# The first expert's first two row tiles, read two batches early and multiplied between the last batch's tasks

## The chip, the cores and the metric

The kernel runs on one core of one Trainium2 chip. The metric is the time of one execution on the device, in microseconds (us). The kernel before takes 782.67 us, the median of 3 runs that lie between 782.0 and 784.62 us. The profile used here is of one execution whose first and last instruction are 782.3 us apart.

Five engines work side by side: TensorE (PE; its weight loads are listed apart as PEld), VectorE (DVE), ScalarE (ACT), GpSimd (POOL) and SyncE (SP, which here only starts transfers). Each works through its own instructions in order and waits on semaphores for the others. 16 DMA engines move the data.

## What is computed

Attention with a sliding window and a linear distance bias, followed by a mixture of experts in which every row goes to one expert.

```python
# attention: q, k, v of (8 batches, 8 heads, 576 positions, 64)
scores = q @ k.T / sqrt(64); bias = -slope[h] * abs(rel)
mask = (rel >= 0) & (rel < 128)
attn = softmax(where(mask, scores + bias, -1e9)); attn_out = attn @ v
# bridge: x of (4608 rows, 512)
logits = x @ w_gate                       # (4608, 8)
expert_idx = argmax(logits, axis=1); gate_w = softmax(logits)[expert_idx]
for e in range(8):                        # w1[e]: (512, 1024), w2[e]: (1024, 512)
    rows = expert_idx == e
    y[rows] = maximum(x[rows] @ w1[e], 0) @ w2[e]
out = gate_w[:, None] * y
```

With the inputs used, the eight experts get 547, 614, 590, 502, 618, 462, 608 and 667 rows. The first expert already has 425 rows after the 27 tiles of 128 rows that the first six batches fill; its 256th row lies in the 16th tile.

## The kernel before

All arithmetic is in float32. The first stage works through 32 units (8 batches x 4 pairs of heads). What turns a finished batch into rows for the experts is a list of tasks (gate logits, transposes, choice of the expert, place of each row, scaling of the row, sending it off); a few tasks are put between the parts of each later unit. Each finished row is written by an indirect DMA into `x_rows`, a table in memory with a stretch for each expert; a row has 512 values, its own number and its gate weight.

```python
def row(ts, i):                      # one tile of 128 rows
    ...
    for hp in range(HP):
        nc.tensor.transpose(m[...], xT[pair][:, hp, c : c + P], ident[:])
    nc.vector.tensor_tensor(xs[:, i % RG, :Dm]..., m[:], rs_all[:, t, :]..., op=ALU.mult)
def send(ts, i):
    scatter(ts[i], xs_of.pop(ts[i])[:, i % RG, :])          # indirect DMA into x_rows
...
for u in range(NU + 1):                                     # NU = 32 units
    ...
    do(0 if slow else 1)
    ...
    do(len(tasks) if u == NU else 0 if slow else 2 if len(tasks) < 14 else 3)
```

The second stage handles 15 groups in turn: for each expert its first 512 rows (4 tiles), and between two experts one tile of 128 rows that some expert has over. A group of 4 tiles is multiplied with Strassen's seven products (`seven1` for the first layer, in two halves, `seven2` for the second); a group of one tile is done plainly (`layer1`, `layer2`).

```python
for i, g in enumerate(groups):
    after = groups[i + 1 : i + 3] + [None, None]
    if after[0] is not None:
        gather(after[0])                              # xg, two buffers: x_rows -> SBUF
        after[0]["w2"] = load_w2(after[0]["src"][1])
    if g["n"] == NJ:
        if i == 0:
            turn(g, [0, 1]); ...                      # the first group's products
            ...                                       # in an order of their own
        seven1(g, 0, ...); seven1(g, 1, ...)
        if i == 0: check_range(first)
    else:
        layer1(g)
    tokens(g)                                         # row numbers, masked -> si
    if after[1] is not None: get_w1(after[1])
    if after[0] is not None:
        turn(after[0], range(after[0]["n"]))          # transposes of the next group's xg
        ...
    if g["n"] == NJ: seven2(g, ...)                   # send_out of its 4 tiles inside
    else: layer2(g)
def send_out(g, j, row):
    ins = nc.gpsimd.indirect_dma_start(
        out=out[:, :], out_offset=bass.IndirectOffsetOnAxis(ap=g["si"][:, j : j + 1], axis=0),
        in_=row, in_offset=None, bounds_check=N - 1, oob_is_err=False)
def tokens(g):                                        # si = (row number & mask0) | mask1
    g["si"] = pools["u"].tile([P, NJ], I32, name="si")
    ...
def gather(g):
    xg = g["xg"] = pools["x"].tile([P, NJ, RW], F32, name="xg")   # bufs=2
    for j0, j1 in ((0, 2), (2, n)) if n > 2 else ((0, n),):
        nc.sync.dma_start(xg[:, j0:j1, :], src[:, j0:j1, :])
```

Of the kernel before, what the change touches and what calls it, by code (L numbers as in the profile page):

```python
# [21 lines left out]
def kernel(  # L22
# [49 lines left out]
    nc.gpsimd.memset(ones_sq[:], 1.0)  # L72
    zero_e = consts.tile([P, E], F32, name="zero_e")
# [51 lines left out]

    def start_routing():
        for sel in sels:
            nc.vector.memset(sel[:], 0.0)
        nc.vector.tensor_copy(sels[n_routed[0] % 2][0:1, :, 0], region[0:1, :])
# [21 lines left out]
    def place(tiles, tmp_pool, ps, name):  # L151
# [17 lines left out]
        if tiles[-1] == NT - 1:  # L169
            nc.vector.tensor_sub(cnt[:], rk[:, :, GT], region[:])  # L170

# [24 lines left out]

    expert_w = {}
# [137 lines left out]

    order_all = ExitStack()
# [12 lines left out]
    k_lo = [P * j for j in range(KT)] + [S - P]  # L349
    with tc.tile_pool(name="tab", bufs=1) as tab, \  # L350
         tc.tile_pool(name="ld", bufs=2) as ld, \
# [8 lines left out]
        rel_i = tab.tile([P, 2 * P], I32, name="rel_i")  # L360
        nc.gpsimd.iota(rel_i[:], pattern=[[1, 2 * P]], base=0, channel_multiplier=-1)
        rel = tab.tile([P, 2 * P], F32, name="rel")
        nc.gpsimd.tensor_copy(rel[:], rel_i[:])
# [3 lines left out]
        for h in range(H):  # L367
            nc.vector.tensor_scalar_mul(fac[:, h, :], rel[:], 2.0 ** (-8.0 * (h + 1) / H))
# [25 lines left out]
        q_sb, k_sb, v_sb, xT, lT, sT = {}, {}, {}, {}, {}, {}  # L394
        probs, exps, mgs, sums = {}, {}, {}, {}

        def load(b):
            q_sb[b] = ld.tile([P, HP, S], F32, name="q_sb")
            k_sb[b] = ld.tile([P, HP, S], F32, name="k_sb")
            v_sb[b] = ld.tile([P, KT + 1, Dm], F32, name="v_sb")  # L400
            cols = slice(b * S, (b + 1) * S)
            step = 1 if b == 0 else HP
            for c in range(0, HP, step):
                nc.sync.dma_start(q_sb[b][:, c : c + step, :], qT3[:, c : c + step, cols])
                nc.sync.dma_start(k_sb[b][:, c : c + step, :], kT3[:, c : c + step, cols])
                if c == 0:
                    nc.sync.dma_start(
                        v_sb[b][:, :KT, :], v[b * S : b * S + KT * P, :].rearrange("(t p) d -> p t d", p=P)
                    )
                    nc.sync.dma_start(v_sb[b][:, KT, :], v[(b + 1) * S - P : (b + 1) * S, :])  # L410

        def scores(u):
# [3 lines left out]
            for j, c, q0, n in BLK:  # L416
                s, c = divmod(c, W // 2)
                for par in range(2):
                    half = slice(par * HALF, (par + 1) * HALF)
                    nc.tensor.matmul(  # L420
                        sps[s][par][:, c : c + n], lhsT=k_sb[b][half, hp, k_lo[j] : k_lo[j] + P],
                        rhs=q_sb[b][half, hp, q0 : q0 + n], start=True, stop=True,
                    )
# [150 lines left out]
        def tasks_of(b):  # L574
# [7 lines left out]
            return ts + [lambda: [send(tiles, i) for i in (len(tiles) - 2, len(tiles) - 1)]]  # L582

        load(0)
        load(1)
# [8 lines left out]
        for u in range(NU + 1):  # L594
# [3 lines left out]
            if u < NU:  # L598
                if hp == 1 and 1 < b + 1 < NB:
                    load(b + 1)  # L600
                if 0 < u <= E:
                    clear_rows(u - 1)
                if u == NU // 2:
                    expert_w[0] = load_w1(moe_w1[0]), load_w2(moe_w2[0])
                scores(u)
                factors(u, 0)
            do(0 if slow else 1)
# [3 lines left out]
            if u > 0:  # L611
# [3 lines left out]
                if hp == 0:  # L615
                    tasks += tasks_of(b - 1)
            do(len(tasks) if u == NU else 0 if slow else 2 if len(tasks) < 14 else 3)

    xe = rte.tile([1, NX], I32, name="xe")
    n_more = rte.tile([1, 3], F32, name="n_more")
    n_more_i = rte.tile([1, 3], I32, name="n_more_i")
    xr = rte.tile([1, NX], I32, name="xr")
    masks = rte.tile([P, 2, E, NJ], I32, name="masks")
    xmasks = rte.tile([P, 2, NX], I32, name="xmasks")

    def extras():
        with tc.tile_pool(name="route", bufs=1) as sm:

            def to_masks(out, has):
                nc.vector.tensor_scalar_mul(out[:, 0], has, -1.0)
                nc.vector.tensor_scalar(
                    out[:, 1], has, scalar1=-float(2 * N), scalar2=float(2 * N), op0=ALU.mult, op1=ALU.add,
                )

            has = sm.tile([P, E, NJ], F32, name="has")
            nc.vector.tensor_tensor(
                has[:], cnt[:].unsqueeze(2).to_broadcast([P, E, NJ]), tail[:, None, :].to_broadcast([P, E, NJ]),
                op=ALU.is_gt,  # L640
            )
            to_masks(masks, has[:])
            og = sm.tile([P, E, NX], F32, name="og")
            nc.vector.tensor_tensor(
                og[:], cnt[:].unsqueeze(2).to_broadcast([P, E, NX]), thr[:, None, :].to_broadcast([P, E, NX]),
                op=ALU.is_gt,
            )
            ovt = sm.tile([P, E], F32, name="ovt")
            nc.vector.reduce_sum(ovt[:], og[:], axis=AX)
            ove = sm.tile([P, E], F32, name="ove")  # L650
            nc.vector.tensor_tensor_scan(ove[:], ovt[:], zero_e[:], 0.0, op0=ALU.add, op1=ALU.add)

            done = sm.tile([P, NX, E], F32, name="done")
            mine = sm.tile([P, NX, E], F32, name="mine")
            k3 = kx[:].unsqueeze(2).to_broadcast([P, NX, E])
            nc.vector.tensor_tensor(done[:], ove[:, None, :].to_broadcast([P, NX, E]), k3, op=ALU.is_le)
            nc.vector.tensor_sub(ovt[:], ove[:], ovt[:])
            nc.vector.tensor_tensor(mine[:], ovt[:, None, :].to_broadcast([P, NX, E]), k3, op=ALU.is_le)
            nc.vector.tensor_sub(mine[:], mine[:], done[:])
            xe_f = sm.tile([1, NX], F32, name="xe_f")  # L660
            nc.vector.reduce_sum(xe_f[:], done[0:1], axis=AX)
            nc.vector.tensor_scalar_min(xe_f[:], xe_f[:], float(E - 1))

            off = sm.tile([P, NX, E], F32, name="off")
            at = sm.tile([P, NX], F32, name="at")
            nc.vector.tensor_sub(off[:], k3, ovt[:, None, :].to_broadcast([P, NX, E]))
            nc.vector.tensor_scalar(off[:], off[:], scalar1=float(NJ), scalar2=float(P), op0=ALU.add, op1=ALU.mult)
            nc.vector.tensor_mul(off[:], off[:], mine[:])
            nc.vector.reduce_sum(at[:], off[:], axis=AX)

            num = sm.tile([P, NX], F32, name="num")
            nc.vector.tensor_mul(mine[:], mine[:], cnt[:, None, :].to_broadcast([P, NX, E]))
            nc.vector.reduce_sum(num[:], mine[:], axis=AX)
            base = sm.tile([P, NX], F32, name="base")
            nc.vector.scalar_tensor_tensor(base[:], in0=num[:], scalar=-float(P), in1=at[:], op0=ALU.add, op1=ALU.min)
            nc.vector.tensor_scalar_max(base[:], base[:], 0.0)
            xr_f = sm.tile([1, NX], F32, name="xr_f")
            nc.vector.scalar_tensor_tensor(
                xr_f[:], in0=xe_f[:], scalar=float(N), in1=base[0:1, :], op0=ALU.mult, op1=ALU.add,
            )  # L680
            nc.vector.tensor_scalar_min(xr_f[:], xr_f[:], float(E * N - P))
            nc.vector.tensor_copy(xr[:], xr_f[:])
            nc.vector.tensor_scalar(base[:], base[:], scalar1=tail[:, 0:1], scalar2=None, op0=ALU.add)
            nc.vector.tensor_tensor(at[:], base[:], at[:], op=ALU.is_ge)
            nc.vector.tensor_tensor(num[:], num[:], base[:], op=ALU.is_gt)
            nc.vector.tensor_mul(num[:], num[:], at[:])
            to_masks(xmasks, num[:])
            nc.vector.tensor_copy(xe[:], xe_f[:])
            nc.vector.tensor_scalar_min(n_more[:, 0:1], ove[0:1, E - 1 :], float(NX))

    def check_range(first):
        with tc.tile_pool(name="range", bufs=1) as sm:
            if first:
                inr = sm.tile([P, NT * H], F32, name="inr")
                n_in = sm.tile([P, 1], F32, name="n_in")
                sums = rs_all.rearrange("p t h -> p (t h)")
# [383 lines left out]
```

## Time and profile before

| what | value |
| --- | --- |
| time, median of 3 | 782.67 us |
| PE busy | 711.7 us (91% of the span) |
| PEld, DVE, ACT, POOL busy | 587.7, 405.3, 220.7, 175.8 us |
| 60 to 195 us (units and tasks) | PE busy 127.06 of 135.00 us |
| 226.5 to 308.4 us (seam, first expert) | PE busy 57.03 of 81.90 us, granted clock 0.83 |
| 439.3 to 504.6 us (one tile over, one expert) | PE busy 64.60 of 65.30 us, granted clock 1.00 |
| moved by DMA | 130.74 MB, mean 167 GB/s |

The page cuts the span into 40 slices of 19.6 us and gives the busy share of each engine in tenths; the row PEclk gives the clock that TensorE was granted, in tenths of full speed. Lines of a timeline give start, duration, engine, source line, operation, tiles and, in brackets, how long the engine had been idle before and what ended that. Lines of a table of waits give the total, the number and the longest of the waits of one kind. A float32 matmul shows as two entries.

### The profile page before, as it was taken

To read this page: it belongs to the slowest core of one execution; us is meant where nothing else is said; L and a number is where in the kernel's file an instruction comes from. 1 tells how busy PE (TensorE), PEld (TensorE's weight loads), DVE (VectorE), ACT (ScalarE), POOL (GpSimd) and SP (SyncE) were. 2 spreads that over 40 slices of the span, in tenths; PEclk is the share of its full clock that TensorE was granted. 3 is DMA by queue.
4 is the path that set the end of the run, shared out by engine and by line. 5 is a ranking of instruction groups with operands and counts; after the bars stand their busy time and mean duration, and the time that the engine had idled before them with its cause. 6 is when DMAs were issued, how large, how long until landed. Compare 5 with 4: busy or idle time off the path is not lost.

```text
span 782.3 us, 11598 instructions
## 1 busy us (share of the span) xinstructions
PE 711.7 (91%) x4678; PEld 587.7 (75%) x4678; DVE 405.3 (52%) x696; ACT 220.7 (28%) x506; POOL 175.8 (22%) x186
## 2 busy tenths in 40 slices
PE   5899899999944879999999999999999999998992
PEld 4677667777634769788788878978878887896881
DVE  4457787777756734463363454436346345443620
ACT  4455555546411112121211212112122121211210
POOL 4446665776630002000200200100020020010001
PEclk9999999999965999999999999999999999999996
DMA  9995895571126021912842482192275348205001
GB/s 332 364 354 195 275 345 168 182 242 56 42 97 245 35 108 41 366 60 89 296 159 108 150 302 108 32 350 76 103 280 175 107 146 308 108 30 189 1 1 58
DMA packets 53615, 130.74 MB, mean 167 GB/s; under 512 B 3503, under 2 KB 3503, under 8 KB 53552
## 3 DMA queue, kind: packets, MB, share of 16 engines
q1 hardware_dynamic: 47024, 110.97, 41.2%
q0 software_dynamic: 6000, 18.92, 6.4%
q8 instruction: 39, 0.64, 0.3%
q14 instruction: 24, 0.20, 0.1%
q10 hardware_dynamic: 528, 0.02, 0.0%
HBM read 102.55 MB, written 28.12 MB: 167 GB/s over the span
## 4 chain that ended last, share of the span: by engine, by line
PE 50%; issue 9%; DMA 5%; DVE 4%; POOL 1%; ACT 1%; SPq 0%; POOLq 0%; DVEq 0%
PE b L783 18%; PE a L783 13%; PE c L783 12%; PE c L941 5%; DMA xg<-x_rows 5%; ACT zo L853 1%; PE tp L909 1%; DVE zo L872 1%; POOL out_dram L880 1%; PE a L909 0%; DMA x_rows<-xs,slots 0%; PE b L909 0%; DVE hs L745 0%; DVE w1s L745 0%; DVE w1s L746 0%
## 5 line engine op out<-in xcount | busy, mean ns | idle before, releaser
L880 POOL DMA_INDIRECT out_dram<-zo,si x32 | 33.8, 1055 | 403.2 <-ACT zo L853 398.3
L420 PE MATMUL sp<-q_sb,k_sb 64*128 64x256 f32 (+2 forms) x640 | 73.0, 373 | 8.9 <-DMA k_sb<-in_kT_dram 5.0
L420 PEld LDWEIGHTS sp<-q_sb,k_sb 64*128 64x128 f32 x640 | 64.0, 202 | 20.5 <-issue 5.6
L427 ACT ACTIVATE e<-sp 128x512 f32<-128x512 f32 x128 | 66.2, 600 | 44.5 <-PE sp L420 44.4
L446 POOL TENSOR_TENSOR mg<-probs 128x768 f32<-128x768 f32 x31 | 57.7, 1860 | 73.2 <-DVE probs L439 37.9
L434 DVE TENSOR_TENSOR probs<-e,fac 128x1024 f32<-128x1024 f32 x32 | 47.0, 1468 | 44.1 <-ACT e L427 29.3
L783 PE MATMUL a<-xgT,w 128*128 128x256 f32 x256 | 62.6, 390 | 7.5 <-DVE xgT L911 7.5
L783 PEld LDWEIGHTS a<-xgT,w 128*128 128x128 f32 x256 | 50.2, 197 | 18.1 <-issue 11.2
L465 PE MATMUL m<-probs,v_sb 128*64 128x256 f32 (+3 forms) x768 | 63.2, 313 | 0.3 <-DVE xs L566 0.2
L783 PE MATMUL b<-xTs,w1s 128*128 128x256 f32 x256 | 60.6, 379 | 0.5 <-DVE u L813 0.5
L853 ACT ACTIVATE zo<-zo,xg 128x256 f32<-128x256 f32 x48 | 21.8, 501 | 136.5 <-DVE zo L864 89.4
L465 PEld LDWEIGHTS m<-probs,v_sb 128*64 128x64 f32 x768 | 47.9, 137 | 16.3 <-issue 2.3
L783 PE MATMUL a<-w,h_sb 128*128 128x256 f32 x256 | 59.3, 386 | 0.0
L783 PE MATMUL b<-w2s,hs 128*128 128x256 f32 x256 | 57.9, 379 | 0.0
L783 PEld LDWEIGHTS a<-w,h_sb 128*128 128x128 f32 x256 | 49.2, 195 | 6.6
L783 PEld LDWEIGHTS b<-xTs,w1s 128*128 128x128 f32 x256 | 48.6, 190 | 7.4 <-DVE u L813 0.9
L783 PEld LDWEIGHTS b<-w2s,hs 128*128 128x128 f32 x256 | 48.6, 190 | 6.6
L941 PE MATMUL c<-w,h_sb 128*128 128x512 f32 x112 | 49.2, 592 | 0.0
L173 POOL DMA_INDIRECT x_rows<-xs,slots x36 | 43.4, 1205 | 19.6 <-DVE cnt L170 8.2
L439 DVE TENSOR_TENSOR probs<-e,fac 128x1024 f32<-128x1024 f32 x32 | 42.3, 1321 | 0.4 <-ACT e L427 0.4
L813 DVE TENSOR_TENSOR u<-b,p 128x512 f32<-128x512 f32 x16 | 11.1, 691 | 52.7 <-PE b L783 52.7
L941 PEld LDWEIGHTS c<-w,h_sb 128*128 128x128 f32 x112 | 20.7, 190 | 23.4 <-issue 23.4
(198 smaller groups left out, 1137.7 us busy)
## 6 DMA issues: line engine op xcount, KB each, us to landing
w<-in_moe_w_dram SPq DMA_DIRECT2D x30, 2048.0 KB, 11.6
x_rows<-zero_row SPq DMA_DIRECT2D x8, 1028.0 KB, 15.0
xg<-x_rows SPq DMA_DIRECT2D x16, 514.0 KB, 4.6
v_sb<-in_v_dram SPq DMA_DIRECT2D x8, 1024.0 KB, 7.9
q_sb<-in_qT_dram SPq DMA_DIRECT2D x7, 1152.0 KB, 7.2
k_sb<-in_kT_dram SPq DMA_DIRECT2D x7, 1152.0 KB, 10.2
v_sb<-in_v_dram SPq DMA_DIRECT2D x8, 256.0 KB, 8.3
xg<-x_rows SPq DMA_DIRECT2D x7, 257.0 KB, 3.8
```

Of the source, the lines that this page charges most:

```text
L173: ins = nc.gpsimd.indirect_dma_start(out=x_d[:, :], out_offset=bass.IndirectOffsetOnAxis(ap=slots[:, t : t + 1], axis=0), in_=row, in_offs ...
L420: nc.tensor.matmul(sps[s][par][:, c : c + n], lhsT=k_sb[b][half, hp, k_lo[j] : k_lo[j] + P], rhs=q_sb[b][half, hp, q0 : q0 + n], start=Tru ...
L427: nc.scalar.activation(exps[u][s][:, par, :], sps[s][par][:], AF.Exp, scale=D ** -0.5)
L434: nc.vector.tensor_tensor(to.rearrange("p a (j c) -> p a j c", c=2 * P), e.rearrange("p a (j c) -> p a j c", c=2 * P), fac[:, heads, None, ...
L439: nc.vector.tensor_tensor(to, e[:], fac2[:, heads, :], op=ALU.mult)
L446: eng.tensor_add(mg[:, :, : 3 * P].rearrange("p a (t c) -> p a t c", c=P), two[:, :, :, 0, :], two[:, :, :, 1, :],)
L465: nc.tensor.matmul(xp[par * HALF : (par + 1) * HALF, lo - q0 : hi - q0], lhsT=v_sb[b][:, j, h * D : (h + 1) * D], rhs=probs[u][:, par, c + ...
L783: nc.tensor.matmul(out_of[:, i, :], lhsT=lhs(i, k), rhs=rhs(k), start=(first and i == 0 and k == 0), stop=(k == nk - 1), skip_group_check= ...
L813: nc.vector.tensor_add(u2[:], bb, p1[:])
L853: nc.scalar.activation(o[:, th, dh, i, :], src[:, i, :], AF.Copy, scale=g["xg"][:, j, Dm + 1 :])
L880: ins = nc.gpsimd.indirect_dma_start(out=out[:, :], out_offset=bass.IndirectOffsetOnAxis(ap=g["si"][:, j : j + 1], axis=0), in_=row, in_of ...
L941: nc.tensor.matmul(zf, lhsT=g["h"][:, fb, :P], rhs=g["w2"][:, fb, :], start=(fb == 0), stop=(fb == FB - 1))
```

## The change

The first expert's group is split. Its first two tiles (256 rows) are read from `x_rows` as soon as the first six batches are in it, two batches before the end, and are multiplied plainly, not with Strassen's products: their first layer between the tasks of the last batch, where TensorE waits, and their second layer after the last task, while the last rows travel to memory and back. The group's other two tiles follow as a plain group of two. If the first expert should have fewer than 256 rows by then, the two tiles are done again at the end.

To make room in SBUF for the new tiles, q and k are loaded for each unit (five buffers) instead of each batch (two buffers). The row numbers for the output are taken straight from the gathered rows (`ids_of_rows`), for all groups but those of one tile; the masks for full groups are gone, because unused rows of the table already hold a number out of range. The single-tile groups get their own transposed tile and hidden layer (`xT2`, `h2`), ACT does all their ReLUs, and the routing sums (`extras`) move ahead of the second stage.

```diff
+    def ids_of_rows(g, j):
+        return g["xg"].bitcast(I32)[:, j, Dm : Dm + 1]
+    def ids_masked(g, j):
+        return g["si"][:, j : j + 1]
     def send_out(g, j, row):
-            out=out[:, :], out_offset=bass.IndirectOffsetOnAxis(ap=g["si"][:, j : j + 1], axis=0),
+            out=out[:, :], out_offset=bass.IndirectOffsetOnAxis(ap=g["ids"](g, j), axis=0),
 ...
+            if tiles[-1] + 1 == early_end:
+                ts.append(lambda: early.update(early_group()))
+        def early_group():
+            g = dict(n=EJ, apart=True, ids=ids_of_rows, xg=plain.tile([P, EJ, RW], F32, name="xg2"))
+            nc.sync.dma_start(g["xg"][:], x_d[: EJ * P, :].rearrange("(j p) r -> p j r", p=P))
+            g["w1"], g["w2"] = expert_w[0]
+            return g
+        def last_tasks():
+            g = early
+            full = lambda: ps_s.tile([P, W // 2], F32, name="sp")
+            turns = [lambda j=j: turn(g, [j], full()) for j in range(EJ)]
+            hid = [lambda fb=fb: layer1(g, fb, ps_m.tile([P, S - 2 * P], F32, name="m")) for fb in range(FB)]
+            ts = tasks_of(NB - 1)
+            more = {2: turns, 6: hid[:3], 8: hid[3:4], 9: hid[4:5], 10: hid[5:6], 11: hid[6:]}
+            for i, task in enumerate(ts):
+                task()
+                for step in more.get(i + 1, ()):
+                    step()
+            extras(tab.tile([P, H, W // 2], F32, name="fac2").rearrange("p h c -> p (h c)"))
+            for j in range(EJ):
+                layer2(g, j, full(), ex.tile([P, 2, W // 2], F32, name="e").rearrange("p a c -> p (a c)")[:, :Dm])
 ...
-            do(0 if slow else 1)
+            do(0 if slow else 1 if b < NB - 1 else 2)
 ...
-            do(len(tasks) if u == NU else 0 if slow else 2 if len(tasks) < 14 else 3)
+            do(0 if slow else 2 if len(tasks) < 14 and b < NB - 1 else 3)
+        do(len(tasks))
+        last_tasks()
 ...
     def experts(first):
+            j0 = EJ if first and e == 0 else 0
             groups.append(dict(
-                n=NJ, e=e, rows=lambda e=e: x_d[e * N : e * N + CAP, :], mask=masks[:, :, e, :], apart=True,
+                n=NJ - j0, e=e, rows=lambda r=e * N + j0 * P, n=NJ - j0: x_d[r : r + n * P, :], ids=ids_of_rows,
+                apart=True,
             ))
 ...
-            tokens(g)
+            if "mask" in g:
+                tokens(g)
```

## The prediction

> **What bounds the kernel now.** I read the page's slices first:
>
> ```profile
> PE   5899899999944879999999999999999999998992
> PEclk9999999999965999999999999999999999999996
> ```
>
> TensorE is full from 40 us on, but for one hole in slices 12 to 14: the seam between attention and experts, where its clock drops too. The busy times by stretch size the hole and show that what follows is dense (columns after the length: PE, PEld, DVE, ACT, POOL, then clock, DMA share, GB/s):
>
> ```profile
> 226.50:308.40 81.90, 57.03 (x247) 48.31 (x247) 41.18 (x82) 11.04 (x20) 4.77 (x7) 0.83 0.29 107
> 373.60:439.30 65.70, 64.72 (x325) 54.86 (x324) 30.02 (x45) 13.51 (x27) 5.22 (x6) 1.00 0.48 167
> ```
>
> PE's waits in the seam:
>
> ```profile
> PE tp L909 <- DMA xg<-x_rows: 10.7, 1, 10.7
> PE a L783 <- DVE xgT L911: 7.5, 1, 7.5
> PE tp L703 <- DVE n_in L701: 4.6, 1, 4.6
> ```
>
> First PE waits for the last rows to reach memory and come back, then for the routing sums on DVE, then for the range check. From 308.4 us on a period (one tile over, then one expert) takes 65.2 to 65.7 us with under 1 us idle. There one more thing must be read: how close the next gather comes to being late. From PE's waits after 310 us and the timeline around 375 us:
>
> ```profile
> PE a L909 <- DMA xg<-x_rows: 3.6, 6, 1.0
> ...
> 374.55 0.91 ACT L853 ACTIVATE zo<-zo,xg 128x256 f32<-128x256 f32 x2 [2.55 <-DVE zo L872]
> 375.48 0.89 SPq L895 DMA_DIRECT2D xg<-x_rows  x2
> 376.80 0.97 POOL L880 DMA_INDIRECT out_dram<-zo,si  x1 [0.30 <-DVE h_sb L933]
> 380.76 1.04 PE L909 MATMUL tp<-ident,xg 128*128 128x128 f32 x8
> 382.78 0.63 PE L909 MATMUL a<-ident,xg 128*128 128x128 f32 x4 [0.98 <-DMA xg<-x_rows]
> 383.68 7.03 PE L941 MATMUL c<-w,h_sb 128*128 128x512 f32 x16
> ```
>
> The gather for the next expert goes out at 375.48, as soon as ACT has used the gate weights in the buffer's old rows. Its first half is just in time for the transposes at 380.76, its second half late by up to 1 us, six times. **The gather has no slack at all.** The fourth send of the old expert starts after it, at 376.80.
>
> **What the Trainium skill says.** "TensorE: Matmul & The Clock Gate", in its part 1 on the HAM clock gate, has PE at half clock after an idle window of about 3.4 us and full again after about as long busy. The trace agrees, and is harsher: after the 2.4 us idle before 222.07 us, 16 transposes at 222.91 took 3.65 us, while 8 take 1.04 at full clock; after 4.6 us idle, 16 matmuls at 282.80 took 5.04 us instead of 3.62. "DMA: Bandwidth & Descriptors", in the anatomy of one DMA on the gpsimd path, puts most of the fixed 2 us into the receipt from memory, without which the semaphore doesn't fire. Agreed: the last scatter starts at 229.63, its data have moved by about 231.9, and it lands at 232.94. "Perfetto Trace Analysis", on the most-contended engine, reads the same bubble repeated for a stretch as a shortage of buffers; that is my worry here.
>
> **The change, part by part.** Prices at full clock, from the timeline: a plain first-layer block of 256 rows is 8 entries of 128x256, as one product (1.73 us); 8 blocks are 13.8 us. The second layer of one tile is 16 entries of 128x512: 6.87 us; of two, 13.7. Transposing two tiles: 1.04.
>
> *Arithmetic.* Strassen for four tiles is 14 x 1.73 + 7 x 3.45 = 48.4 us; plain, twice 27.5 = 55.1. So PE gets 6.7 us more work.
>
> *The tail of attention.* The last unit's matmuls end at about 215.9 us. In the built order follow two logits (1.4), 8 early transposes (1.0), the gate's transposes (1.6), a row (0.45), three first-layer blocks (5.2), then the placing of rows, where PE waited 2.4 us before and now doesn't: about 225.7. Placing (0.7), four rows (0.45 each), three blocks between them and two after: 225.7 + 0.7 + 1.8 + 5 x 1.73 = 236.9, against 226.6 before. The second layer then runs to L = 250.6.
>
> *The wait for the rows.* It should lie behind that second layer, but doesn't. In the built program the gather of tiles 2 and 3 waits for the two early sends of outputs to land (its buffer lies where their tiles lay). So after L: ACT's weighing 0.15 + 0.69, POOL 0.15 later, landing 3.4 (the scatter at 229.63 took 3.31, the one at 225.72 3.5), SP's start 0.43 (232.94 to 233.37), gather 3.85 (233.37 to 237.22): PE starts at 259.3, at half clock.
>
> *Tiles 2 and 3.* Transposes 1.9 (as at 237.22), last copy 0.9, first layer 13.8 + 0.7 for the slow clock, one tile's transposes 0.5, second layer 13.7: the first tile over starts at 259.3 + 31.5 = 290.8. Before: 308.4. **Saved: 17.6 us.** The waits for DVE's sums are gone, because plain products need none; the sums for expert two run behind a single tile's work, and its w1 has been asked for 14 us earlier.
>
> *What it adds everywhere.* `ids_of_rows` makes each send read its row numbers from `xg` itself. A buffer that a transfer reads can't be overwritten until the transfer has landed, and in the built program the gather of each next expert now waits for all four sends of the last one, where before it waited for ACT and for `si`. So in each period the gather goes out not at 375.48 but at 376.80 + 3.4 + 0.43 = 380.6: 5.1 us later, on a transfer without slack. First half at 380.6 + 3.9 = 384.5 instead of 380.76: PE idles 3.7 us, enough to lose its clock. Four tiles' transposes at half clock take 3.8, so the single tile's second layer starts at 388.4 to 388.7 instead of 383.68: **4.9 us for each of six experts, 29.4 us.** For the second expert only one send comes after the last matmul: gather out at T + 1.0 + 3.4 + 0.43, first half at T + 8.7, where PE is ready at T + 7.15; with the half clock, 2.3 us.
>
> *No time:* masks removed, ReLUs moved, own tiles for single-tile groups (nothing in PE's waits names them), loads by unit (four units ahead, 18 us in the fast first units, against 7 to 10 us from issue to landing; after the first matmul PE never waits for q or k). The redo at the end doesn't run: 425 rows are there, 256 needed.
>
> Sum: 782.7 - 17.6 + 2.3 + 29.4 = 796.8.
>
> **Rivals.**
> 1. *The seam is all that counts* (the sends land in time, or one slow gather is absorbed): 782.7 - 17.6 = 765; if moreover the wait for rows did hide behind the second layer, 757. For it: the seam is the only hole in the page. Against it: the wait is in the built order, and six late second halves show that nothing is left to absorb.
> 2. *The send lands later than I think.* The median of all sends is 6.7 us to landing, the worst 8.5. Those ran beside weight loads; in the new order gather and weights wait behind the sends, so 3.4 to 4.2 (an early send of the last expert took 4.2) is what I choose. At 4.2, 0.8 more in seven places, 802; at 6.7, about 820.
> 3. *The tail doesn't fill.* DVE or POOL bounds the last two units, with five tasks a unit (PE waited 8.1 us in all for POOL's `mg`), or early loads collide with the clearing of `x_rows`: a few us more, 800 to 803.
>
> **Range and chances.** The per-period price dominates: 3.5 to 6.5 us gives 788 to 806. The seam's saving I trust to 4 us. Taken together I predict 797, 787 to 807. The line of 2% slower lies at 798.3, 1.5 us above my sum, so same and slower are nearly even; the errors that I can name lean upward, but the sum lies below. Faster by 2% needs rival 1.
>
> **What would show it.** Right: PE's waits hold about six of 3.5 to 5 us on the gather and a clock below 1.0 after each; SP waits for landed sends, not for ACT; periods of about 70 us instead of 65.3; the first single tile near 291 us, after 8 to 9 us idle between early second layer and the transposes of tiles 2 and 3. Wrong: periods still at 65, which would mean that the wait ends earlier than the landing; or a hole before 237 us, which would mean that the tail isn't filled.

## The result and the profile after

The changed kernel takes 787.53 us, the median of 4 runs (786.75 to 788.78), against 782.46 us for the kernel before on the same chip. The ratio is 1.0061, with a 95% interval of 1.0038 to 1.0084. The change costs about 5 us, a third of the 14.3 us that were predicted; the time lies at the lower edge of the predicted range (787 to 807 us). In the two profiled executions the spans differ by 3.2 us (785.5 against 782.3), and the sums below refer to these.

Most of the hole in the seam is closed, and small holes have opened behind it. The slices of the page:

```profile
PE   5899999999798799998999899899989989998992
PEclk8999899999999699999999999999999999999996
```

The two slices with a 4 have gone. From slice 19 on, every few slices an 8 stands among the 9s, where before there was none until the fourth slice from the end. The busy times by stretch of the changed kernel (the columns as in the prediction's table) give both sizes:

```profile
226.50:293.00 66.50, 57.63 (x204) 37.99 (x202) 17.36 (x50) 8.59 (x19) 9.03 (x10) 0.90 0.38 139
359.10:428.40 69.30, 66.42 (x325) 56.02 (x324) 28.70 (x39) 14.49 (x31) 5.28 (x6) 0.98 0.45 159
428.40:497.30 68.90, 66.35 (x325) 56.52 (x324) 28.69 (x39) 14.49 (x31) 5.25 (x6) 0.98 0.45 159
```

The seam up to the first single tile (a tile over from some expert) ends at 293.0 us instead of 308.4. The two periods shown, each from one single tile to the next, take 69.3 and 68.9 us where the same two took 65.7 and 65.4 before, with 2.9 and 2.6 us without a matmul and a clock of 0.98. PE's waits from 226 to 790 us:

```profile
PE tp L441 <- DMA xg<-x_rows: 23.6, 8, 7.9
PE a L450 <- DVE xT L443: 0.9, 1, 0.9
PE a L441 <- DMA xg<-x_rows: 0.7, 2, 0.4
```

The waits for the last rows, for DVE's sums and for the range check (10.7, 7.5 and 4.6 us before) have become one of 7.9 us in the seam, and the other seven of the first line are new: 0.7 us for the second expert and 2.3 to 2.6 us for each of six later ones. What SP's gathers (`xg`) wait for, from 300 us on, names the cause:

```profile
SPq L981 <- DMA out_dram<-zo,xg: 153.0, 7, 30.0
...
SPq L981 <- ACT zx L462: 64.8, 6, 11.6
```

In the kernel before, the first of these lines was

```profile
SPq L895 <- ACT zo L853: 164.3, 7, 26.7
```

that is, the weighing of the rows with the gate on ACT. Now it is the landing of a send, a transfer to the output. The total means nothing, because SP has little else to do; what counts is the releaser. The timeline of one period of the changed kernel shows the order:

```profile
360.05 0.91 ACT L950 ACTIVATE zo<-zo,xg 128x256 f32<-128x256 f32 x2 [2.55 <-DVE zo L969]
...
362.30 0.98 POOL L416 DMA_INDIRECT out_dram<-zo,xg  x1 [0.30 <-ACT h L454]
...
365.24 0.89 SPq L981 DMA_DIRECT2D xg<-x_rows  x2
...
368.99 1.11 PE L441 MATMUL tp<-ident,xg 128*128 128x128 f32 x8 [2.56 <-DMA xg<-x_rows]
```

ACT has used the gate weights at 360.96, as in the kernel before; yet the gather leaves at 365.24, after the fourth send (362.30) has landed. Its input now has the name `zo,xg`: the send reads the row numbers from the gathered rows.

### The profile page after: what moved, and what is told of

The parts are those of the page before. It is cut to its first block, busy times and chain, and to the rows that moved or that the text cites. A ratio compares the mean times of both kernels' runs of the same rounds, so it can differ in the third digit from the quotient of the medians.

```text
span 785.5 us, 11571 instructions
## 1 busy us (share of the span) xinstructions
PE 720.9 (92%) x4646; PEld 585.1 (74%) x4646; DVE 367.8 (47%) x618; ACT 225.8 (29%) x535; POOL 175.1 (22%) x186
## 4 chain that ended last, share of the span: by engine, by line
PE 67%; issue 13%; DVE 6%; DMA 5%; POOL 4%; ACT 3%; SPq 0%; POOLq 0%; DVEq 0%
PE b L880 16%; PE a L880 11%; PE c L880 11%; PE a L458 6%; PE sp L550 5%; PE m L595 5%; DMA xg<-x_rows 4%; PE sm L614 2%; PE m L693 1%; DMA out_dram<-zo,xg 1%; PE a L450 1%; PE m L450 1%; PE tp L441 1%; DVE probs L564 1%; PE b L450 1%
## 5 line engine op out<-in xcount | busy, mean ns | idle before, releaser
L416 POOL DMA_INDIRECT out_dram<-zo,xg x28 | 29.7, 1060 | 325.6 <-ACT zo L950 321.3
L458 PE MATMUL a<-w,h 128*128 128x512 f32 x128 | 56.9, 597 | 0.0
L880 PE MATMUL a<-xgT,w 128*128 128x256 f32 x224 | 53.0, 379 | 0.0
L880 PE MATMUL b<-xTs,w1s 128*128 128x256 f32 x224 | 52.9, 379 | 0.0
L880 PE MATMUL a<-w,h_sb 128*128 128x256 f32 x224 | 50.6, 379 | 0.0
L880 PE MATMUL b<-w2s,hs 128*128 128x256 f32 x224 | 50.6, 379 | 0.0
L880 PEld LDWEIGHTS a<-xgT,w 128*128 128x128 f32 x224 | 42.5, 190 | 8.7 <-issue 3.3
L880 PEld LDWEIGHTS a<-w,h_sb 128*128 128x128 f32 x224 | 42.1, 190 | 5.5
L458 PEld LDWEIGHTS a<-w,h 128*128 128x128 f32 x128 | 24.2, 194 | 27.1 <-issue 27.1
L441 PE MATMUL tp<-ident,xg 128*128 128x128 f32 x92 | 16.4, 329 | 23.6 <-DMA xg<-x_rows 23.6
```

What stands on the lines that cost most here:

```text
L416: ins = nc.gpsimd.indirect_dma_start(out=out[:, :], out_offset=bass.IndirectOffsetOnAxis(ap=g["ids"](g, j), axis=0), in_=row, in_offset=No ...
L441: nc.tensor.transpose(tp[:, db * P : (db + 1) * P], g["xg"][:, j, db * P : (db + 1) * P], ident[:])
L458: nc.tensor.matmul(ps[:], lhsT=g["h"][:, fb, j * P : (j + 1) * P], rhs=g["w2"][:, fb, :], start=(fb == 0), stop=(fb == FB - 1),)
L880: nc.tensor.matmul(out_of[:, i, :], lhsT=lhs(i, k), rhs=rhs(k), start=(first and i == 0 and k == 0), stop=(k == nk - 1), skip_group_check= ...
```

## The experiments

The excerpts of edits below are shortened. The theory: two changes are mixed here. The early tiles shorten the seam, and the row numbers taken straight from `xg` keep that buffer busy until the last send has landed, which delays every later gather. One rival: the delay comes from other things that the change brings to the later periods (the q and k buffers, ReLUs on ACT, own tiles for single-tile groups). A second rival: the direct reading itself is slow, not the buffer's lifetime.

**Row numbers copied first, the rest as changed.**

```diff
 def tokens(g):
+    if "mask" not in g:
+        g["si"] = pools["u"].tile([P, NJ], I32, name="si4")
+        nc.vector.tensor_copy(g["si"][:, : g["n"]], bits[:, : g["n"], Dm])
+        return
-    ... ids=ids_of_rows          # groups of 4 and 2 tiles
+    ... ids=ids_masked
```

> The changed kernel, but the groups of four and of two tiles copy their row numbers into a small tile of their own (one DVE copy, 0.15 us), and the sends read that. Nothing else differs. Theory (the gather of each next expert waits until the old expert's sends have landed, because they read their row numbers from the gathered rows): 3.1 us fewer in each of six periods and 0.7 for the second expert, so 787.5 - 18.5 = 769 us (766 to 772), periods back at 65.3 us, PE without a wait over 1 us on the gather, SP released by ACT. Rival (the periods got longer by something else that the change does to the second stage: all ReLUs on ACT, own tiles for the single-tile groups, another order of loads): 785 to 788 us, periods still near 68.5.

Measured: 766.3 us, ratio to the kernel before 0.9797 (0.978 to 0.9813). PE's waits from 226 us on in this kernel:

```profile
PE tp L441 <- DMA xg<-x_rows: 8.1, 2, 7.9
PE a L441 <- DMA xg<-x_rows: 3.6, 5, 1.2
```

What SP's gathers wait for, from 300 us on, is ACT again:

```profile
SPq L981 <- ACT h L454: 138.5, 6, 23.1
```

The seven new waits have shrunk to one of 0.2 us; what remains is the seam's 7.9 us and the late second halves of the kernel before. One copy on DVE per group returns about 21 us. The span falls from 785.5 to 766.9.

**The kernel before with the row numbers read directly, and nothing else of the change.**

```diff
+        ids = g["si"][:, j : j + 1] if g["n"] == 1 else g["xg"].bitcast(I32)[:, j, Dm : Dm + 1]
-            out=..., out_offset=bass.IndirectOffsetOnAxis(ap=g["si"][:, j : j + 1], axis=0),
+            out=..., out_offset=bass.IndirectOffsetOnAxis(ap=ids, axis=0),
-            tokens(g)
+            if g["n"] == 1: tokens(g)
```

> The kernel before, with this one part of the change done alone: the sends of the four-tile groups read their row numbers from the gathered rows, and the masking into a small tile is left out for them. Theory: each of seven gathers waits for four landed sends, 3.1 us each: 782.5 + 21.7 = 804 us (799 to 808). Rival (the row numbers cost nothing; the loss comes with the other parts): 782 us within 0.3%.

Measured: 811.24 us, ratio 1.0391 (1.0364 to 1.0419). That is 29 us over its neighbour of 782.02 us, about 4 for each of seven experts, and above the 799 to 808 us expected. SP's waits from 330 us on in this kernel:

```profile
SPq L896 <- DMA out_dram<-zo,xg: 180.8, 8, 31.0
```

and PE's waits in the same stretch:

```profile
PE tp L910 <- DMA xg<-x_rows: 16.8, 6, 3.7
```

The direct reading alone brings the new releaser and the new waits, so the first rival falls. The cost per period is 3.8 us in the profile, more than the 3.1 expected: the clock dropped at the transposes in six of the seven periods.

**The changed kernel with the gathered rows in two buffers.** The sends still read their row numbers directly. The second half of the rows, whose sends come last, lies in a buffer of its own.

```diff
-        xg = g["xg"] = pools["x"].tile([P, NJ, RW], F32, name="xg")
+        xh = [pools["x"].tile([P, 2, RW], F32, name="xh")]      # tiles 2, 3: loaded first
+        xg = pools["x"].tile([P, 2, RW], F32, name="xg")        # tiles 0, 1
```

> The changed kernel with the sends still reading their row numbers from the gathered rows, but the gathered rows of a group lie in two tiles of two row tiles each; the second of them has both of its buffers for the large groups alone. Theory (what costs is how long a buffer stays in use, not that the sends read it): the first half's gather waits only for the first two sends, which start 3.4 us before the last, so it goes out 2.7 us after the single tile begins and lands before PE needs it at 7.15; the second half is there early. No stall in the six periods, and the 3.6 us of late second halves that remained with copied row numbers go too: 763 us (761 to 766). Rival (a send that reads its row numbers from the gathered rows slows the sends or the gathers in itself): over 775 us.

Measured: 764.47 us, ratio 0.9758 (0.9733 to 0.9783). The timeline of SP in one period of this kernel:

```profile
334.80 1.37 SPq L988 DMA_DIRECT2D xh<-x_rows  x1
361.41 0.37 SPq L990 DMA_DIRECT2D xg<-x_rows  x1
```

and of POOL:

```profile
358.53 0.98 POOL L416 DMA_INDIRECT out_dram<-zo,xg  x1 [0.30 <-issue]
360.51 1.17 POOL L416 DMA_INDIRECT out_dram<-zo,xh  x1 [1.00 <-ACT zo L956]
361.98 0.98 POOL L416 DMA_INDIRECT out_dram<-zo,xh  x1 [0.30 <-ACT h L460]
```

The gather still waits for a send: 361.41 is 2.88 us after the start of the second one at 358.53. But that send comes early enough, and the last one (361.98) holds up only `xh`, which is not needed at that moment: its rows were fetched 26 us before into the other copy of the buffer. PE waits 0.8 us in all on gathers after 300 us. The period that begins here takes 64.55 us (358.80 to 423.35), exactly what it takes with copied row numbers in the same two buffers (347.32 to 411.87 in the first kernel under "All together" below). So the second rival falls as well: what costs is how long the buffer lives, not the direct reading.

**Early outputs in a place of their own.** This goes on from the copied row numbers, and also moves the two early outputs out of the memory that the next gather needs.

```diff
+            zo2 = rows.tile([P, 2 * S], F32, name="lT", bufs=1)
-                layer2(g, j, full(), ex.tile([P, 2, W // 2], F32, name="e")...[:, :Dm])
+                layer2(g, j, full(), zo2[:, j * Dm : (j + 1) * Dm])
```

> As the run with copied row numbers, and the early tiles' outputs lie where the last batch's logits lay instead of where the gather of tiles 2 and 3 will write. Theory (that gather waits for the early sends to land, only because of the place): it goes out when the last scatter has landed, near 239.5 us, and is hidden behind the early second layer; the 7.9 us of idle and about 3 us of half clock after it go: 769 - 11 = 758 us (755 to 762). Rival (the wait moves on to the routing sums, the weights of the first single tile or the rows themselves): 765 to 769 us.

Measured: 756.67 us, ratio 0.968 (0.9664 to 0.9696); its interval lies below that of the copied row numbers alone. The timeline of this kernel's seam:

```profile
234.96 0.97 POOL L178 DMA_INDIRECT x_rows<-xs,slots  x1 [1.69 <-DVE fac L372]
236.74 13.90 PE L458 MATMUL sp<-w,h 128*128 128x512 f32 x32
238.90 0.38 SPq L982 DMA_DIRECT2D xg<-x_rows  x1
...
251.41 1.09 PE L441 MATMUL tp<-ident,xg 128*128 128x128 f32 x8 [0.78 <-ACT lT L462]
```

The gather leaves as soon as the last row has landed, behind the early second layer, and the transposes follow that layer after 0.78 us at full clock. The first single tile starts at 281.51 us, 26.9 us earlier than in the kernel before; 1.1 us of this were there already when unit 27 began. This is what the early tiles can do once nothing else waits for their outputs.

**How much of the seam is due to plain products?** The kernel before, with the first expert's four tiles multiplied plainly at their old place, so nothing is early and no sums are needed:

```diff
-    if i == 0: turn(g, [0, 1]); ...; seven1(...)       # Strassen, sums on DVE
+    if i == 0: turn(g, range(NJ)); 8 blocks of 512 rows, plain; later 4 tiles of layer 2, plain
```

> The kernel before, with the first expert's four tiles multiplied plainly after all rows are in, nothing early: 6.7 us more arithmetic on PE, but no waits for DVE's sums. Theory (much of the seam's gain is that plain products need no sums): tile transposes to about 242 us behind the routing sums, then 27.5 + 0.5 + 27.5 us and 2 us for half clock: the first single tile at about 299.5 instead of 308.4 us, so 773.5 us (771 to 777). Rival (the gain of 15.4 us is all from working early): 6.7 us more arithmetic shows, 782 to 789 us.

Measured: 773.2 us, ratio 0.9893 (0.9877 to 0.991): 8.8 us less, though it gives PE 6.7 us more work by the prediction's count. PE's waits from 220 to 320 us in this kernel:

```profile
PE tp L909 <- DMA xg<-x_rows: 10.3, 1, 10.3
PE m L158 <- DVE gsum L558: 2.4, 1, 2.4
PE a L995 <- DVE xgT L911: 1.7, 1, 1.7
```

The wait for the rows is as before; the 7.5 us for the sums have become 1.7, and the 4.6 us for the range check are gone. The first single tile starts at 297.17 us, 11.2 us earlier than before, 1.0 of them there already at unit 27. So more than half of the 15.4 us that the seam gained needed no early reading at all.

**Row length and the landing.** The prediction took 3.4 us for a send to land, read off the scatters into `x_rows`. In the changed kernel five sends that a gather waited for land in 2.67 to 2.76 us. A scattered row has 514 values, 2,056 bytes; a sent row has 512, 2,048 bytes. Is it the odd length? The kernel before with rows of 528 values, 2,112 bytes:

```diff
-    RW = Dm + 2
+    RW = Dm + 16
```

> The kernel before with rows of 528 instead of 514 values in the table (2112 instead of 2056 bytes; the added values hold copies of the gate weight and are not used). It asks why I took a send's landing for 3.4 us when it took 2.5: I took it from a scatter into the table, whose rows end in a piece of 8 bytes, where a send writes 2048 bytes. Theory (the short last piece makes the receipt late by about 1 us): from the start of the last scatter on POOL to SP's start of the gather about 2.9 us instead of 3.74, and 781.2 us in all. Rival (scatters land later for another reason, such as the five in a row): 3.7 us still, 782 us.

Measured: 782.89 us, ratio 0.9993 (0.9979 to 1.0006), so no gain in time. But the chain of work that ended last, in this kernel (start, duration, what), has

```profile
229.26 2.75 DMA x_rows<-xs,slots
```

where the same chain of the kernel before has

```profile
229.63 3.31 DMA x_rows<-xs,slots
```

and that of the changed kernel has, for the fourth send of the period that begins at 428.40 us,

```profile
431.58 2.75 DMA out_dram<-zo,xg
```

The longer row lands 0.56 us sooner than the shorter one, and SP's gather starts 3.18 us after the scatter instead of 3.74, where 2.9 was expected. Two more kernels of this section also have rows of 2,056 bytes and the same last scatter: it lands in 3.45 us with direct reading and in 3.09 with plain products. The DMA records of the traces tell where the difference arises. The last packet of each of these four scatters has ended 2.37 to 2.38 us after the start; from there to the landing it is 0.94, 1.07 and 0.71 us with 2,056 bytes and 0.37 with 2,112. Those five sends of the changed kernel have 0.33 to 0.37, the slowest in the kernel before with direct reading 0.56. The packets hold two whole rows each, so the short last piece of the theory is not seen. That scatters were a bad model for sends because of their row length, and not because of what they write to, rests on one profile with the longer rows; which property of 2,056 bytes matters was not tried.

**Pace of the tasks.** The change works off tasks faster in the last batches. Set back to the pace of the kernel before, first with the early outputs in their own place:

```diff
-            do(0 if slow else 1 if b < NB - 1 else 2)
+            do(0 if slow else 1)
-            do(0 if slow else 2 if len(tasks) < 14 and b < NB - 1 else 3)
+            do(0 if slow else 2 if len(tasks) < 14 else 3)
```

> As the run with copied row numbers and the early outputs in another place, but the tasks of the last batch's units are paced as before the change (three in a unit, not five). Theory (five tasks a unit crowd POOL, whose merge of the last but one unit then comes up to 2 us late): 1.5 us less, 755 us (754 to 756). Rival (the pace doesn't matter or the old one delays the early rows): 756.5 us or more.

Measured: 754.17 us, ratio 0.9626 (0.9603 to 0.9649), 2.5 us below the 756.67 us at the new pace. These two kernels were not run side by side, but their ratios to the kernel before have intervals that don't overlap. Their profiled spans (754.4 and 753.9 us) don't show the gain: in that profile of the old pace, unit 27 began 1.8 us later (180.66 against 178.88), and from there to the first single tile it took 2.1 us less.

**All together.** Copied row numbers, the early outputs' own place and two buffers, at the new pace:

> The run with copied row numbers and the early outputs in another place, with the gathered rows in two tiles as well. Theory: the late second halves (3.6 us in PE's waits) go: 756.7 - 3.6 = 753 us (751.5 to 755). Rival (the wait moves to the weights, which are asked for in the same queue): 756 us.

Measured: 752.28 us, ratio 0.9609 (0.9582 to 0.9635). And the same once more, beside its twin at the old pace:

> The same kernel as the one with two buffers and the faster pacing, on the chip of its old-pacing twin, so that the two are set side by side: 752 us if the earlier figure holds; the difference to the twin is what the pacing is worth, 1 to 2.5 us by the first theory, under 0.5 us by the second.

> This is the changed kernel with the early outputs in a place of their own, the gathered rows in two buffers, and the task pacing of the kernel before (one task per unit, then two or three). Two theories on the pacing. If the faster pacing of the change is what ends the attention 1.5 us later (217.4 against 215.9 us in the two profiles), the old pacing gives that back and takes nothing else: 752.28 - 1.5 = 751 us, with the first single tile of the first expert about 1 us earlier. If the pacing is indifferent, because work moved from the tail to the units costs what it saves, the time stays at 752 to 754 us. The run with the old pacing and one buffer (754.17 us against 756.67 us with the faster pacing) speaks for the first, by 2.5 us in time, though its profiled span did not show it.

Measured: 751.33 us (0.9575 to 0.9644) and **747.13 us (0.9523 to 0.9614)**, 35 us below the kernel before. The intervals of these two overlap, so the whole times don't settle what the pace is worth. The stage does. In the timeline of PE, the scores of unit 27 and the logits after the last unit, at the new pace,

```profile
178.63 2.06 PE L556 MATMUL sp<-q_sb,k_sb 64*128 64x256 f32 x20
...
216.20 1.25 PE L641 MATMUL m<-xT,wgb 128*32 128x256 f32 x16
```

and at the old one:

```profile
177.18 2.06 PE L556 MATMUL sp<-q_sb,k_sb 64*128 64x256 f32 x20
...
212.54 1.25 PE L641 MATMUL m<-xT,wgb 128*32 128x256 f32 x16
```

The last units take 37.57 us at the new pace and 35.36 at the old one. Of the six profiles at the new pace, five have 37.56 or 37.57 us for this stretch (that of the changed kernel is one) and that of the direct reading in two buffers has 39.20; the six at the old pace have 34.83 to 36.09, with 36.09 in the kernel before. The tail does not pay it back: from these logits to the first single tile it is 65.07 us in both twins. So the faster pace costs 2.2 us in these twins. The 1.45 us by which unit 27 starts earlier in the second twin come from further up, where the paces are the same, and belong to no edit.

## Why the prediction was wrong

**The mechanism was right.** The seam saves, each period pays, through the wait for the landed sends that the prediction named. Undoing the direct reading gives 766.3 us, close to the 765 us of the first rival, so that rival is what the kernel would have been with one copy. What failed is the size of the term repeated six times.

| step | predicted | measured in the changed kernel |
| --- | --- | --- |
| first single tile | 290.8 us (17.6 saved) | 293.00 us (15.4 saved) |
| second expert | +2.3 us | +0.9 us |
| gather of a period later by | 5.1 us | 4.2 us |
| PE idle before the transposes | 3.7 us | 2.3 to 2.6 us |
| first transpose to second layer | 3.9 to 4.2 us | 2.3 to 3.4 us, mean 3.0 |
| each of six periods | +4.9 us | five periods +3.12 on average, the last +2.1 to the end |
| sum | +14.1 us | -15.4 + 0.9 + 5 x 3.12 + 2.1 = +3.2 us |

The last period costs less because the kernel before lost 2.06 us at the same transposes.

**The term that failed: 4.9 us for each of six experts.** It was mis-sized in two places.

*The landing.* From the start of the fourth send to the gather I took 3.4 + 0.43 = 3.83 us; the timeline above has 362.30 to 365.24, 2.94 us. I had read the landing off a transfer with rows of another length, and SP's start off a moment when it took twice as long (0.43 us against 0.21 here). The trace of the kernel before held a better model. Its view of the sends, from which the prediction's second rival has the 6.7 and 8.5 us, also gives the shortest:

```profile
DMA to landing us min/median/max: 2.9/6.7/8.5
```

That is the send at 568.33 us, which landed before the next gather went out at 571.94. In the new order the gather waits for the sends, so they too run without it. The second rival erred on the other side: the six gathers left 5.8 to 6.2 us after the single tile's start, none later than the 7.0 that I had worked out. The landing is worth about 0.9 us in each of seven places. The second expert's step loses the rest of its 2.3 us because its transposes kept the full clock (8 in 1.07 us at 301.02).

*The clock.* I took half clock for all transposes in every period; that is the other half of the 1.8 us by which 4.9 was too much. "TensorE: Matmul & The Clock Gate", in its part 1 on the HAM clock gate, says that the activity window runs freely, so that the point of change depends on where in it the work falls. The trace fits this, though it doesn't show the window, and the prediction should have taken the drop as a chance and not as a certainty. In the timeline of PE in the changed kernel, two neighbouring periods:

```profile
438.26 1.97 PE L441 MATMUL tp<-ident,xg 128*128 128x128 f32 x8 [2.55 <-DMA xg<-x_rows]
...
507.05 1.09 PE L441 MATMUL tp<-ident,xg 128*128 128x128 f32 x8 [2.42 <-DMA xg<-x_rows]
```

Two of the six periods keep the full clock and cost 2.4 and 2.5 us over the same periods of the kernel before; three start at half clock, one drops during its transposes, and these cost 3.5 to 3.7 us where the next single tile follows. In the kernel before with direct reading, eight transposes started at full clock (1.09 us) after 2.54 us idle and at half clock (1.97 us) after 2.51, so no fixed length of idle time divides the two.

**The seam** was right within 2.2 us, by terms that partly cancel. The last unit ends 1.5 us later than I took (217.4 against 215.9): the faster pace, which the prediction listed under rival 3 and left out of the sum. From the second early send to the gather it is 2.98 us (252.60 to 255.58) where I took 3.83. And the slow clock after the 7.9 us idle lasted longer: the timeline of PE has

```profile
259.53 1.94 PE L441 MATMUL tp<-ident,xg 128*128 128x128 f32 x8 [7.93 <-DMA xg<-x_rows]
262.41 3.75 PE L450 MATMUL a<-xT,w 128*128 128x256 f32 x8 [0.94 <-DVE xT L443]
265.95 2.68 PE L450 MATMUL b<-xT,w 128*128 128x256 f32 x8
268.47 1.89 PE L450 MATMUL c<-xT,w 128*128 128x256 f32 x8
```

The two blocks start 3.54 and 2.52 us before their successors instead of 1.73 each: 2.6 us lost, where I gave 0.7.

**Right as predicted:** the transposes of tiles 2 and 3 at 259.53 (259.3), 7.9 us idle before them (8 to 9), SP waiting for landed sends, six similar waits on the gather, and no cost from the rest of the change in the experts: with the row numbers copied, PE's waits on gathers after the seam are those of the kernel before, but for 0.2 us.

## What to carry to other kernels

In these kernels a transfer that takes its addresses from a buffer holds that buffer until it has landed. Before saving a small copy, see who refills the buffer and whether that refill has slack; if not, keep the copy, or split the buffer so that the last reader holds only what is needed last. And when a predicted cost is multiplied by the number of periods, take its duration from the very kind of transfer, with the same row length and the same traffic beside it, and weigh a clock drop by its chance.

## What was not expected of the hardware

Rows of 2,056 bytes took 3.09 to 3.45 us from the indirect DMA's start to its landing in three profiles, rows of 2,112 bytes 2.75 us in one, and rows of 2,048 bytes 2.67 to 2.76 us in five sends of the changed kernel. "DMA: Bandwidth & Descriptors", in the anatomy of one DMA, puts most of the fixed 2 us into the write receipt and fits the whole as 2.0 us plus bytes over 436 GB/s. For the 128 rows of each of these transfers that is an estimate of 2.6 us at all three lengths. Two of them lie near it; the middle length lies 0.5 to 0.85 us above, for which the fit has no term.

The measurement also differs on where the fixed part lies. The changed kernel's send at 252.60 us ran behind no other: by the DMA records its first packet starts 1.54 us after the send, its last has ended after 2.37, and it lands after 2.72. So 0.35 us follow the last packet, and most of the rest comes before the first. The prediction's "Agreed" was too quick: in its own example, the scatter at 229.63, 0.94 of 3.31 us follow the last packet.
